# Decode block on one core: the stored row as one transfer of two rows, V in four loads, b1 in two

## The chip, the cores and the metric

The kernel runs on one core of one Trainium2 chip. The metric is the device time of one execution in microseconds (us). A profile of one execution is at hand as well; its *span*, from the first to the last instruction, is a little shorter than the time that is measured for that same execution.

## What is computed

One token `x` of 1024 numbers goes through an attention block over a sliding window and, beside it, through a small feed-forward block; both results are added to `x`.

```python
xn = layernorm(x)                                   # 1024
# A: 32 query heads of 128, 4 key/value heads, the last W = 4096 rows of the caches
q  = (xn @ wq)                                      # wq: 1024 x 4096
p  = softmax(q . k_cache[:, Sk-W:] / sqrt(128))     # K window: 4 x 4096 x 128
o  = p @ v_cache[:, Sk-W:]                          # V window: 4 x 4096 x 128
A  = o.reshape(4096) @ wo                           # wo: 4096 x 1024
# B
h  = gelu(layernorm(xn) @ w1 + b1)                  # w1: 1024 x 3584, b1: 3584
B  = h @ w2 + b2                                    # w2: 3584 x 1024
out = x + A + B                                     # 1024 numbers, bfloat16
```

All inputs are bfloat16. Every weight and both cache windows are read once: about 39.9 MB in all, for one token.

## The kernel before

The whole kernel is one straight program without loops at run time. All large inputs come over SyncE's (SP's) DMA queue, in this order: K in four loads of 1 MB, one for each key head (L76); wq in two loads of 4 MB (L85); w1 in one load of 7 MB (L200); V in three loads, the first with two heads (2 MB) and the others with one (L208); w2 in one load of 7 MB (L214); wo in one load of 4 MB and five smaller ones of 2 MB down to 256 KB (L222). ScalarE's (ACT's) own DMA queue carries four small loads near the start: x in two layouts (L107, L108), b2 (L109) and b1 as eight rows of 448 numbers, 896 bytes each (L110). The tile `b1_8` that receives b1 is read by two matmuls at L238, which put b1 into the accumulator `acch` before the products with w1 (L243) are added there.

SBUF holds only part of the weights at a time, so the loads wait for one another's buffers. The pool `big` has two buffers of 64 KB per partition: the first takes K and the first half of wq (`kq`), and later w1 (`w1t`); the second takes the transposed K (`kt2`), and later w2 (`w2t`). The pool `ring` has two buffers of 32 KB: the second half of wq and V, then the two halves of wo. So w1 is issued when the first half of the wq products (L231, the 32 matmuls that read `kq`) is done; w2 when the scores (L260) are done; the second half of wo when `o_all` (L296, 32 matmuls on V) is done.

The stages in order: VectorE (DVE) transposes K block by block (L185) and moves the blocks together with ACT (L194, L196). TensorE (PE) makes q (L231), turns it (L247), makes the scores (L260); then come the maximum, the exponential (L275), the feed-forward's first product (L243) and GELU (L288), the product with V (L296), and at the end one long chain of 112 matmuls and a tail of 16 that accumulate w2 and wo rows into the result (L323, L340). The result lies as two rows of 512 numbers, in partitions 0 and 32. DVE and ACT write them to the tile `res` (L344, L345), and they are stored by two DMAs of one row each, one issued by SP (L347) and one by ACT (L348). At the end SP waits until every DMA has reported (L374), and the engines meet in a barrier.

Two things set the order of the work that the source leaves open:

- The framework's planner orders each engine's instructions ahead of time. It goes through the program with its own estimate of when things are ready, and an engine takes, of what is ready by that estimate, what stands first in the source. So the two matmuls of L238, which stand behind L231 in the source, run ahead of it; and L247 and L260 run ahead of L243, which stands before them. On the chip every engine then runs its instructions strictly in the order planned.
- DMAs issued by SP and ACT report on eight completion counters, handed out in turn over both queues, in the planned order. A DMA is not issued before the DMA that used its counter last, eight places ahead, has landed. The order is: K (4 loads), x, x, b2, b1, then wq (2), w1, V (3), w2, wo (6), and the two stores. So the two loads of wq wait for the first and the second load of K, although their buffers are free.

Of the kernel before, what the change touches and what calls it, by code (L numbers as in the profile page):

```python
# [15 lines left out]
def kernel(  # L16
# [14 lines left out]
    nc = tc.nc  # L31
    P = 128
    D = A_x.shape[-1]
    Hkv = A_k_cache.shape[1]
    Sk = A_k_cache.shape[2]
# [5 lines left out]
    W = min(4096, max(256, Sk // 4))  # L41
# [24 lines left out]
    def big_tile(name):  # L66
        return big.tile([P, 2 * RING_ELEMS], BF16, tag="big", name=name, align_bytes=256)
# [35 lines left out]
    x32 = consts.tile([32, 32], BF16)  # L103
    xb8 = consts.tile([8, 256], BF16)
    b1_8 = consts.tile([8, NH], BF16)
    with tc.issue_after(first_exp.ins):
        nc.scalar.dma_start(out=x32[:], in_=x_flat.rearrange("(a n) -> a n", a=32))  # L107
        nc.scalar.dma_start(out=xb8[0:4, :], in_=x_flat.rearrange("(a n) -> a n", a=4))  # L108
        nc.scalar.dma_start(out=xb8[4:8, :], in_=B_b2.rearrange("(a n) -> a n", a=4))  # L109
        nc.scalar.dma_start(out=b1_8[:], in_=B_b1.rearrange("(a n) -> a n", a=8))  # L110
    zf = consts.tile([P, 512 + Hq], FP32)
    nc.gpsimd.memset(zf[:], 0.0)
    zeros = zf[:, 0:512]
# [73 lines left out]
    for R in range(4):  # L187
        for Cd in range(4):
            src = scr[32 * R:32 * R + 32, :, :].rearrange("p g (c a j) -> p g c a j", a=4, j=32)[:, :, :, Cd, :]
            dst = kT[32 * Cd:32 * Cd + 32, :, WQ4 * R:WQ4 * (R + 1)].rearrange("p g (c j) -> p g c j", j=32)  # L190
            moves.append((dst, src))
    for i, (dst, src) in enumerate(moves):
        if i % 3 == 2:
            nc.scalar.copy(out=dst, in_=src)  # L194
        else:
            nc.vector.tensor_copy(out=dst, in_=src)  # L196

    w1t = big_tile("w1t")
    w1v = w1t[:, :C * Fd].rearrange("p (r n) -> p r n", r=C)
    nc.sync.dma_start(out=w1v, in_=w1_v)  # L200
# [2 lines left out]
    q_sb = q_f.rearrange("p (b n) -> p b n", b=2)  # L203
    v_sb = ring_tile("v_sb")
    v4 = v_sb[:].rearrange("p (g c d) -> p g c d", g=Hkv, c=NCH)
    for g0, g1 in ((0, 2), (2, 3), (3, 4)):
        src = A_v_cache[0, g0:g1, Sk - W:Sk, :].rearrange("g (p c) d -> p g c d", p=P)
        nc.sync.dma_start(out=v4[:, g0:g1, :, :], in_=src)  # L208

    chunk_src = []  # L210
    w2_v = B_w2.rearrange("(p c) n -> p c n", p=P)
# [14 lines left out]
    for i, w3 in enumerate(wq_tiles):  # L226
        for r in range(4):
            c = 4 * i + r
# [19 lines left out]
    for b in range(2):  # L248
        src = qT_ps[:, b * 4:(b + 1) * 4, :].rearrange("p hh (th t f) -> p th t hh f", th=2, t=2)[:, :, :, :, 0]
# [93 lines left out]
    res = consts.tile([33, 512], BF16)  # L343
    nc.vector.tensor_tensor(out=res[:, 0:N1], in0=acct[0][0:33, :], in1=bulk[0][:], op=ALU.add)  # L344
    nc.scalar.copy(out=res[:, N1:512], in_=acct[1][0:33, :])  # L345
    out_v = out.rearrange("a b (t n) -> (a b t) n", t=2)
    nc.sync.dma_start(out=out_v[0:1, :], in_=res[0:1, :])  # L347
    nc.scalar.dma_start(out=out_v[1:2, :], in_=res[32:33, :])  # L348


# [28 lines left out]
```

## Time and profile before

| what | us |
|---|---|
| median of 3 runs (lowest, highest) | 101.81 (101.69, 101.94) |
| the profiled execution's own time | 101.68 |
| its span, first to last instruction | 100.0 |
| PE busy, 361 matmuls | 48.5 |
| DVE busy | 38.2 |
| ACT busy | 29.2 |
| DMA: 39.91 MB moved, mean over the span | 399 GB/s |

Busy times are of one execution. The share of a whole span says little about a single stage; which wait ends last in a stage says more. About 1.7 us of the execution's time lie outside the span (101.68 against 100.0).

### The profile page before, as it was taken

Reading aid. Unit: us, or ns where it says so; the run is one execution under the profiler, and the core shown is the slowest. Engines: PE = TensorE matmul, PEld = TensorE weight load, DVE = VectorE, ACT = ScalarE, POOL = GpSimd, SP = SyncE. Lnnn points to the kernel's source line nnn. Section 1 sums busy time; section 2 is a strip of 40 time slices with the busy share of each in tenths; the row PEclk is TensorE's granted clock in tenths of the full one; section 3 lists DMA queues with packets and bytes.
Section 4 is the critical chain, followed back from the end, with each engine's and each line's share of the span. In section 5 each row is a group of like instructions: output and inputs, shape, how many; then the busy total and the mean of one; then the engine's idle time right before and its main releaser. Section 6 shows DMA issues by size and latency. Waiting matters only on the chain.

```text
span 100.0 us, 913 instructions
## 1 busy us (share of the span) xinstructions
PE 48.5 (49%) x361; PEld 19.5 (20%) x361; DVE 38.2 (38%) x26; ACT 29.2 (29%) x34; POOL 8.6 (9%) x33
## 2 busy tenths in 40 slices
PE   0006400008500940089149407997100999999980
PEld 0003100002100300053126203342000234224320
DVE  0069999999999970010631051002400000000020
ACT  5306100007999999900150440000400000000010
POOL 7911560000000000000001000000000000000000
PEclk9999999999995555555966997599755569999997
DMA  2999999999999888998599998998899999999910
GB/s 26 387 420 431 456 502 459 446 433 433 420 420 577 367 367 367 482 620 367 213 420 436 426 534 390 459 620 351 367 413 393 420 420 420 420 426 415 398 53 1
DMA packets 2663, 39.91 MB, mean 399 GB/s; under 512 B 338, under 2 KB 356, under 8 KB 740
## 3 DMA queue, kind: packets, MB, share of 16 engines
q1 hardware_dynamic: 2578, 39.85, 93.5%
q8 instruction: 3, 0.05, 0.2%
q10 hardware_dynamic: 82, 0.01, 0.1%
HBM read 39.86 MB, written 0.00 MB: 399 GB/s over the span
## 4 chain that ended last, share of the span: by engine, by line
DMA 80%; PE 14%; SPq 2%; issue 1%; DVE 0%
DMA v_sb<-in_A_v_cache_dram 33%; DMA wo<-in_A_wo_dram 25%; DMA kq<-in_A_wq_dram 17%; PE o_all L296 9%; DMA kq<-in_A_k_cache_dram 5%; PE accq L231 4%; SPq L222 1%; PE acct L340 1%; SPq L208 1%; DVE res L344 0%; PE acct L336 0%; SPq L200 0%
## 5 line engine op out<-in xcount | busy, mean ns | idle before, releaser
L194 ACT COPY kt<-kt 32x4096 bf16<-32x4096 bf16 x5 | 18.0, 3602 | 10.4 <-DVE kt L185 10.3
L185 DVE STREAM_TRANSPOSE kt<-kq 128x4096 bf16<-128x4096 bf16 x4 | 17.4, 4413 | 5.8 <-DMA kq<-in_A_k_cache_dram 5.8
L196 DVE COPY kt<-kt 32x4096 bf16<-32x4096 bf16 x11 | 13.4, 1219 | 0.2
L323 PE MATMUL accf<-w2t 128*1 128x512 bf16 x56 | 8.3, 466 | 5.7 <-DMA w2t<-in_B_w_dram 5.7
L296 PE MATMUL o_all<-v_sb,w1t 128*32 128x512 bf16 x32 | 8.8, 442 | 4.3 <-DMA v_sb<-in_A_v_cache_dram 4.3
L329 DVE COPY bulk<-accf 33x320 f32<-33x320 f32 x1 | 0.5, 482 | 24.7 <-ACT bulk L328 24.7
L231 PE MATMUL accq<-kq,xnT 128*1 128x512 bf16 x32 | 3.6, 627 | 10.2 <-DMA kq<-in_A_wq_dram 10.2
L323 PE MATMUL accf<-wo,o 128*1 128x512 bf16 x56 | 7.5, 378 | 0.1
L328 ACT COPY bulk<-accf 33x192 f32<-33x192 f32 x1 | 0.3, 312 | 23.2 <-PE accf L323 23.2
L231 PE MATMUL accq<-wq,xnT 128*1 128x512 bf16 x32 | 3.6, 626 | 6.1 <-DMA wq<-in_A_wq_dram 6.1
L231 PEld LDWEIGHTS <-xnT 128*1 128x1 bf16 x64 | 2.1, 116 | 20.5 <-issue 20.5
L296 PEld LDWEIGHTS <-w1t 128*32 128x32 bf16 x32 | 3.4, 109 | 9.6 <-DVE w2t L291 4.7
L323 PEld LDWEIGHTS <-w2t 128*1 128x1 bf16 x56 | 2.8, 98 | 10.8 <-issue 8.7
L243 PE MATMUL acch<-w1t,yT 128*1 128x448 bf16 x64 | 4.5, 450 | 0.0
L299 DVE TENSOR_TENSOR o_m<-o_all,grs 32x512 f32<-32x512 f32 x1 | 0.7, 678 | 9.0 <-PE o_all L296 9.0
L139 PE MATMUL x_ps<-x,zb 32*128 32x8 bf16 x4 | 0.2, 162 | 7.9 <-DMA x<-in_A_x_dram 7.9
L247 PE MATMUL qT_ps<-zb,w1t 128*128 128x128 bf16 x8 | 1.0, 311 | 6.2 <-ACT w1t L233 6.2
L303 ACT CAST o_bf<-o_f 32x128 bf16<-32x128 f32 x1 | 0.3, 297 | 12.5 <-DVE o_f L301 12.5
L291 DVE STREAM_TRANSPOSE w2t<-w1t 128x896 bf16<-128x896 bf16 x1 | 1.7, 1700 | 5.7 <-ACT w1t L288 5.7
L260 PE MATMUL sp<-kt,zb 128*32 128x512 bf16 x32 | 3.7, 631 | 0.3 <-DVE zb L252 0.3
L321 PE MATMUL spare<-zf,ident_f 128*1 128x512 f32 x8 | 3.6, 592 | 0.0
L323 PEld LDWEIGHTS <-o 128*1 128x1 bf16 x56 | 2.6, 82 | 4.3 <-issue 1.1
(78 smaller groups left out, 40.3 us busy)
## 6 DMA issues: line engine op xcount, KB each, us to landing
w1t<-in_B_w_dram SPq DMA_DIRECT2D x1, 7168.0 KB, 24.3
w2t<-in_B_w_dram SPq DMA_DIRECT2D x1, 7168.0 KB
kq<-in_A_k_cache_dram SPq DMA_DIRECT2D x4, 1024.0 KB, 8.1
kq<-in_A_wq_dram SPq DMA_DIRECT2D x1, 4096.0 KB, 17.1
wq<-in_A_wq_dram SPq DMA_DIRECT2D x1, 4096.0 KB, 24.1
wo<-in_A_wo_dram SPq DMA_DIRECT2D x1, 4096.0 KB
v_sb<-in_A_v_cache_dram SPq DMA_DIRECT2D x1, 2048.0 KB, 28.6
v_sb<-in_A_v_cache_dram SPq DMA_DIRECT2D x2, 1024.0 KB, 30.6
```

The source lines that it names most:

```text
L185: nc.vector.transpose(out=scr[:, g, :], in_=k2[:, g, :])
L194: nc.scalar.copy(out=dst, in_=src)
L196: nc.vector.tensor_copy(out=dst, in_=src)
L208: nc.sync.dma_start(out=v4[:, g0:g1, :, :], in_=src)
L222: nc.sync.dma_start(out=tv[:, a:b, :], in_=wo_v[:, nr * i + a:nr * i + b, :])
L231: nc.tensor.matmul(accq[32 * t:32 * t + 1, b, :], lhsT=xnT[:, c:c + 1], rhs=w3[:, r, j * 512:(j + 1) * 512], start=(c == 0), stop=(c == C ...
L243: nc.tensor.matmul(acch[32 * t:32 * t + 1, b, :NH], lhsT=yT[:, c:c + 1], rhs=w1v[:, c, j * NH:(j + 1) * NH], start=False, stop=(c == C - 1 ...
L260: nc.tensor.matmul(sp[32 * R:32 * R + 32, a, :], lhsT=qm[:, g, :], rhs=kT[:, g, c0:c0 + 512], start=(g == 0), stop=(g == Hkv - 1), tile_po ...
L291: nc.vector.transpose(out=hT, in_=h_sb.rearrange("p (d c) -> p c d", c=CW2))
L296: nc.tensor.matmul(o_all[:].rearrange("h g d -> h (g d)"), lhsT=eTb[:, 32 * c:32 * c + 32], rhs=v4[:, :, c, :], start=(c == 0), stop=(c == ...
L321: nc.tensor.matmul(spare[0:1, :], lhsT=ident_f[:, 0:1], rhs=zeros, start=True, stop=True)
L323: last = nc.tensor.matmul(accf[32 * half:32 * half + 1, :], lhsT=vec[kind](c), rhs=wap[:, half * 512:(half + 1) * 512], start=False, stop= ...
```

## The change

The result is stored by one DMA from SP that takes partitions 0 and 32 of `res` as two rows; the store from ACT goes. V is loaded by four loads of one head each instead of three. b1 is loaded by two DMAs of four rows: the first from ACT as before, the second from SP, and in the source it stands just ahead of w1's load.

```diff
     b1_8 = consts.tile([8, NH], BF16)
+    b1_v = B_b1.rearrange("(a n) -> a n", a=8)
     with tc.issue_after(first_exp.ins):
         nc.scalar.dma_start(out=x32[:], in_=x_flat.rearrange("(a n) -> a n", a=32))
         nc.scalar.dma_start(out=xb8[0:4, :], in_=x_flat.rearrange("(a n) -> a n", a=4))
         nc.scalar.dma_start(out=xb8[4:8, :], in_=B_b2.rearrange("(a n) -> a n", a=4))
-        nc.scalar.dma_start(out=b1_8[:], in_=B_b1.rearrange("(a n) -> a n", a=8))
+        nc.scalar.dma_start(out=b1_8[0:4, :], in_=b1_v[0:4, :])
...
+    nc.sync.dma_start(out=b1_8[4:8, :], in_=b1_v[4:8, :])
     w1t = big_tile("w1t")
     w1v = w1t[:, :C * Fd].rearrange("p (r n) -> p r n", r=C)
     nc.sync.dma_start(out=w1v, in_=w1_v)
...
-    for g0, g1 in ((0, 2), (2, 3), (3, 4)):
-        src = A_v_cache[0, g0:g1, Sk - W:Sk, :].rearrange("g (p c) d -> p g c d", p=P)
-        nc.sync.dma_start(out=v4[:, g0:g1, :, :], in_=src)
+    for g in range(Hkv):
+        nc.sync.dma_start(out=v4[:, g, :, :], in_=A_v_cache[0, g, Sk - W:Sk, :].rearrange("(p c) d -> p c d", p=P))
...
     out_v = out.rearrange("a b (t n) -> (a b t) n", t=2)
-    nc.sync.dma_start(out=out_v[0:1, :], in_=res[0:1, :])
-    nc.scalar.dma_start(out=out_v[1:2, :], in_=res[32:33, :])
+    nc.sync.dma_start(out=out_v, in_=res[0:33:32, :])
```

## The prediction

> **What bounds the kernel now.** I read the page first, then the chain that ended last, then a table of stretches, SP's own issues and waits, and last the start and the end of the timeline. From the page, the slices and the DMA queues:
>
> ```profile
> span 100.0 us, 913 instructions
> DMA  2999999999999888998599998998899999999910
> q1 hardware_dynamic: 2578, 39.85, 93.5%
> q8 instruction: 3, 0.05, 0.2%
> q10 hardware_dynamic: 82, 0.01, 0.1%
> ```
>
> The 16 DMA engines are full from the second slice to the 38th. SP's queue (q1) alone takes 93.5% of their time over the whole span. The table of stretches says it again, its last two columns being DMA share and GB/s:
>
> ```profile
> 3.00:26.00 23.00, 5.95 (x44) 2.68 (x45) 20.18 (x7) 5.61 (x14) 5.71 (x22) 1.00 1.04 445
> 26.00:36.00 10.00, 3.89 (x40) 0.94 (x31) 9.89 (x9) 9.96 (x4) 0.00 (x0) 0.72 0.92 400
> 36.00:60.00 24.00, 10.10 (x113) 5.76 (x109) 5.15 (x8) 10.24 (x9) 0.53 (x2) 0.69 1.03 441
> 60.00:95.00 35.00, 26.50 (x154) 9.54 (x156) 2.03 (x3) 1.12 (x4) 0.00 (x0) 0.80 0.99 422
> 95.00:100.00 5.00, 2.06 (x24) 0.60 (x20) 0.96 (x2) 0.62 (x2) 0.00 (x0) 0.87 0.08 25
> ```
>
> (The shares a little over 1 and 0.92 offset each other: long packets are booked where they start.) So from 3 to 95 us the time is the bytes. The chain of waits has steps that look like compute:
>
> ```profile
> 27.87 32.50 DMA v_sb<-in_A_v_cache_dram
> 60.50 8.77 PE o_all L296 x32
> 70.58 25.00 DMA wo<-in_A_wo_dram
> 95.62 0.60 PE acct L340 x8
> 97.22 0.48 DVE res L344
> ```
>
> The 8.77 us of `o_all` are in this chain only because they release the buffer of wo's last five loads. Those then wait 25 us behind w2 and the first half of wo, which are still in the queue; `o_all` could be many microseconds later at no cost. What sets the end is the stream of bytes, whose last landing is at 96.8, and the 3.2 us of the span (100.0 - 96.8) that follow it. An edit can move the time in three ways: it makes the stream longer, lets it run dry, or changes what follows it. The stream runs dry if SP issues a load too late:
>
> ```profile
> 8.42 0.33 SPq L85 DMA_DIRECT2D wq<-in_A_wq_dram  x1
> 26.50 0.33 SPq L200 DMA_DIRECT2D w1t<-in_B_w_dram  x1
> 26.87 1.42 SPq L208 DMA_DIRECT2D v_sb<-in_A_v_cache_dram  x3
> 47.56 0.33 SPq L214 DMA_DIRECT2D w2t<-in_B_w_dram  x1
> 97.78 0.32 SPq L347 DMA_DIRECT2D out_dram<-res  x1
> ```
>
> wq's second load lands 24.1 us after its issue, at 32.5; w1 is issued at 26.50, 6 us ahead. That is the tightest margin: w2 (47.56) has until V's last landing at 60.4.
>
> **V in four loads.** One more issue on SP of 0.47 (1.42 / 3): it ends near 28.8 instead of 28.3, and SP has nothing to issue before 47.56, so it is hidden. In the stream, bytes and packets stay (rows of 8 KB either way, 1152 such packets in the trace with those of K and wo), and 16 completion writes of 9 ns are added, one for each engine. The cost of a boundary between loads is bounded from the rows: w1 lands at 50.8 (26.50 + 24.3), V's first 2 MB at 55.5 (26.87 + 28.6), so 4.7 or 2.35 for each MB; the two that follow land at 57.9 (27.36 + 30.6) and 60.37, 2.43 each. A boundary costs at most 0.08; the 9 ns packet is the lower end. I take 0.02, since engines' own landings in the middle of the 16 differ by only that.
>
> The Trainium skill's page "DMA: Bandwidth & Descriptors", section "Rules for kernel authors", says the opposite of splitting: coalesce many small transfers, below 64 KB one pays mostly overhead; its section "Anatomy of one DMA" puts the constant at about 2 us each (there for DMAs issued from GpSimd). By that, as an estimate, the added V load and b1 load would make the time 4 us longer. The 2.43 us between landings of 1 MB, in which the packets alone need 8 x 0.309 = 2.47 for each engine, contradict it for loads queued behind one another.
>
> **b1 in two.** ACT's issue of 0.33 becomes about 0.26 (L109 has four rows), on an engine that next waits for x. The other half goes into SP's queue behind wq. Its counter is the one of K's third load, which landed at 10.7, so SP issues it near 10.7 (0.33) and then reaches w1, for which it waits until 26.50 anyway: hidden. Four of the engines carry a packet of 41 ns and one of 9 ns more and four others less: -0.05 to +0.05 on the stream, and I take +0.03. What counts is when it lands: behind 8 MB of wq, near 32.6 instead of 9.3 for the whole of b1 now. Its only reader is L238:
>
> ```profile
> 9.78 0.92 PE L238 MATMUL acch<-b,zb 8*128 8x448 bf16 x2
> 12.12 0.59 PE L150 MATMUL ln_tot<-st,ones_f 128*128 128x2 f32 x2 [1.42 <-ACT sq L148]
> ```
>
> Today it sits early on PE, ahead of the second layernorm and of the wq products (22.88 and 32.56). The planner has to place it anew. It puts an instruction where its operands are due: L247 and L260 run at 42.4 and 43.7, ahead of L243, which comes first in the source but has to wait for w1. On SP the b1 half stands behind wq's second load, so it is due just after that, when the second 32 matmuls of L231 (first in the source) are ready as well. So I expect L238 behind them, at 36.1 (32.56 + 3.58), where PE is idle for 6.2 us until L247 at 42.37. Its 0.92 us are hidden there; 9.78 to 10.7, where it was, was idle time too, so nothing is gained.
>
> **One store.** The end today, from SP's waits and the timeline:
>
> ```profile
> 97.78 0.25 ACTq L348 DMA_DIRECT2D out_dram<-res  x1
> SPq L347 <- DVE res L344: 25.8, 1, 25.8
> SPq L374 <- DMA out_dram<-res: 0.7, 1, 0.7
> ```
>
> Both stores are issued together. In the trace's packets they go through one DMA engine, at 98.515 (ACT's) and 98.561 (SP's); they report at 98.90 and 99.08. SP checks the counters in turn, ACT's and then SP's; it is past the last check at 99.22. The new store issues from SP at 97.78 as well. Issue: 0.32 with one row; the nearest rows for a few rows are 0.26 (L109) and 0.57 (L108), the farthest end is 0.87 (a wo load); I take 0.32. From issue to report: 1.12 (ACT's) to 1.30 (SP's, behind the other); I take 1.25, as a single DMA has nothing ahead of it on its engine. Its counter is the next after those of today's stores, which is the last that SP checks: one step of 0.06 fewer behind the report. So -0.11, between -0.31 (issue 0.25, report after 1.12, one step) and +0.49 (issue 0.87, the report as late as today, one step fewer).
>
> The same page, section "Why a DMA increments its semaphore by 16 and not by 1", says that a DMA runs on the largest number of engines up to 16 that divides its slowest dimension: two for two rows, four for half of b1. q10's 82 packets agree: 49 rows, and 16 + 4 + 4 + 8 + 1 completion writes.
>
> **The sum.** 101.68 + 0.02 + 0.03 - 0.11 = 101.62 for the profiled execution. That lies 0.13 below the median of the runs, so 101.75 as a median. No change that can be told: a measurement of this kernel can tell about 0.3%, or 0.3 us.
>
> **Rivals.**
>
> - *L238 keeps its place* ahead of the wq products (slower). Then PE stands at L238 until 32.6, and behind it 0.59 of layernorm and 3.61 of L231, which release w1: 32.6 + 0.92 + 0.59 + 3.61 = 37.7 instead of 26.49. The queue is empty from 32; from SP's first issue (0.79) to the first packet (1.82) pass 1.0, so the stream stands from 32 to 38.7. 101.75 + 6.7 = 108.4. It decides once w1's issue falls behind about 31. For it: that is the place today, and the half lands 23 us later than b1 does now. Against it: the planner's rule as the trace shows it. 0.15.
> - *The store is dearer*: two rows take an issue like L108 or the wo load, and the time becomes up to 101.75 + 0.6 = 102.35. 0.10.
> - *Two late engines become one*: three fetches of 16 KB of instructions (q8) run through the DMA engines, 0.96 us each, at 48.8 and 69.2 and at the end. Two of the 16 engines report wo's last load at 96.8, the others by 95.7. If another program layout puts both fetches on one engine, 1 us more: 102.75. Nothing in the diff changes PE's count of instructions by more than a wait or two. 0.06.
> - *A fixed cost for each transfer*: each of the two added loads stops the stream for as long as the store takes from issue to report, 1.3 us: 101.75 + 2.6 = 104.35. Against it are V's landings. 0.03. (The two sections named above are the rule for this.)
> - *The end gains more*: all lower bounds of the store hold, and the half of b1 costs nothing: 101.75 - 0.31 = 101.45 or, with the spread between runs, 101.2. This is the only gain I see. 0.22.
> - *The change isn't what it says*: bytes, packets and order of the large loads are the same, so most of it is nothing; that is in my forecast.
>
> **How the numbers follow.** Forecast (no change) 0.44: 101.45 to 102.1. Faster 0.22, down to 101.2. Slower 0.15 + 0.10 + 0.06 + 0.03 = 0.34. A range from 101.2 to 102.9 holds 0.44 + 0.22 + 0.10 + 0.06 = 0.82 and leaves out the stall and the fixed cost.
>
> **What would show it.** Right: q1 with 2578 + 16 + 8 + 2 = 2604 packets and q10 with 82 - 8 - 2 = 72; L238 near 36 us, waiting for nothing long; w1 issued at 26.5; DMA share as today in every stretch up to 95; `o_all` still starting near 60.5; the store's report between 98.9 and 99.1. Wrong: L238 ahead of L231 and w1 issued near 37, with slices of the DMA row near 0; V's landings more than 2.5 us apart; or a last wo landing that is not at 96.8.

## The result, and the profile after

| kernel | median us (lowest, highest) | ratio to before, 95% interval |
|---|---|---|
| before | 101.78 (101.61, 101.94), 10 runs | |
| changed | 101.98 (101.90, 102.24), 10 runs | 1.0026 [1.0018, 1.0035] |

The change makes the kernel 0.2 us slower. That is inside the range that was given and below the 0.3% that was called the limit, but the interval leaves out 1: ten runs of each tell it from no change. The sum had pointed the other way, to -0.06.

The profiled execution after took 102.24, the highest of its ten. Its page, the slices and the queues:

```profile
span 100.4 us, 913 instructions
...
DMA  2999999999999889998699999988899998999900
...
q1 hardware_dynamic: 2604, 39.85, 93.2%
...
q10 hardware_dynamic: 72, 0.01, 0.1%
```

The stream is as full as it was, and the two packet counts, 2604 and 72, are those that the prediction worked out. SP's issues and, in the second fence, PE's start:

```profile
10.63 0.33 SPq L199 DMA_DIRECT2D b<-in_B_b_dram  x1
26.45 0.35 SPq L202 DMA_DIRECT2D w1t<-in_B_w_dram  x1
26.85 1.85 SPq L209 DMA_DIRECT2D v_sb<-in_A_v_cache_dram  x4
47.55 0.33 SPq L215 DMA_DIRECT2D w2t<-in_B_w_dram  x1
...
97.94 0.57 SPq L348 DMA_DIRECT2D out_dram<-res  x1
```

```profile
12.07 0.59 PE L151 MATMUL ln_tot<-st,ones_f 128*128 128x2 f32 x2 [2.27 <-ACT sq L149]
22.82 3.58 PE L232 MATMUL accq<-kq,xnT 128*1 128x512 bf16 x32 [10.16 <-DMA kq<-in_A_wq_dram]
32.51 3.58 PE L232 MATMUL accq<-wq,xnT 128*1 128x512 bf16 x32 [6.10 <-DMA wq<-in_A_wq_dram]
36.02 0.92 PE L239 MATMUL acch<-b,zb 8*128 8x448 bf16 x2
```

The half of b1 is issued at 10.63, and its two matmuls (L239 now) moved to 36.02, behind both halves of the wq products. w1 goes out at 26.45 as before. The only row that departs from what was expected is the last of SP's: the store's issue takes 0.57 us where one row took 0.32. The end of the chain that ended last, then one of SP's waits:

```profile
95.81 0.60 PE acct L341 x8
96.41 0.42 PE acct L337 x4
96.83 0.53 PE acct L341 x6
...
97.38 0.48 DVE res L345
```

```profile
SPq L374 <- DMA out_dram<-res: 0.8, 1, 0.8
```

The store begins 0.56 after the last DVE operation begins, just as before (97.94 - 97.38; 97.78 - 97.22). In the trace's completion counts it reports at 99.56, 1.62 after its issue began; before, the two stores reported 1.12 and 1.30 after theirs.

This profile's DVE operation also starts 0.16 later than the one before did (97.38 against 97.22). That can't be put down to the change: over the kernels below the same row starts anywhere from 97.07 to 97.38, in single profiles, and in e4, which has the same loads, at 97.15.

### The profile page after: what moved, and what is told of

Its sections match the earlier page's. It is cut to its first block, busy times and chain, and to the rows that moved or that the text cites. A ratio compares the mean times of both kernels' runs of the same rounds, so it can differ in the third digit from the quotient of the medians.

```text
span 100.4 us, 913 instructions
## 1 busy us (share of the span) xinstructions
PE 47.7 (48%) x361; PEld 19.6 (20%) x361; DVE 38.2 (38%) x26; ACT 29.2 (29%) x34; POOL 8.6 (9%) x33
## 3 DMA queue, kind: packets, MB, share of 16 engines
q1 hardware_dynamic: 2604, 39.85, 93.2%
## 4 chain that ended last, share of the span: by engine, by line
DMA 81%; PE 12%; SPq 2%; issue 1%; DVE 0%
DMA v_sb<-in_A_v_cache_dram 32%; DMA wo<-in_A_wo_dram 27%; DMA kq<-in_A_wq_dram 17%; PE o_all L297 7%; DMA kq<-in_A_k_cache_dram 5%; PE accq L232 4%; SPq L209 1%; PE acct L341 1%; SPq L223 1%; DVE res L345 0%; PE acct L337 0%; SPq L202 0%
## 5 line engine op out<-in xcount | busy, mean ns | idle before, releaser
L297 PE MATMUL o_all<-v_sb,w1t 128*32 128x512 bf16 x32 | 7.1, 379 | 3.9 <-DMA v_sb<-in_A_v_cache_dram 3.9
L244 PEld LDWEIGHTS <-yT 128*1 128x1 bf16 x64 | 3.1, 107 | 1.4
```

Of the source, the lines that this page charges most:

```text
L244: nc.tensor.matmul(acch[32 * t:32 * t + 1, b, :NH], lhsT=yT[:, c:c + 1], rhs=w1v[:, c, j * NH:(j + 1) * NH], start=False, stop=(c == C - 1 ...
L297: nc.tensor.matmul(o_all[:].rearrange("h g d -> h (g d)"), lhsT=eTb[:, 32 * c:32 * c + 32], rhs=v4[:, :, c, :], start=(c == 0), stop=(c == ...
```

## The experiments

All kernels of a group (e1 to e4, e5 to e7, e8 to e10) ran on one chip beside the kernel before, each group on another chip; the two probes ran once each. A number that serves all of them is the *ending*: from the start of the last DVE operation (`res`) to the end of the last instruction, read from one profiled execution of each kernel. It holds the store and nothing of the stream.

| kernel | result row(s) stored by | ratio to before | ending us |
|---|---|---|---|
| before | SP and ACT, one row each | | 99.97 - 97.22 = 2.75 |
| changed | SP, partitions 0 and 32 | 1.0026 | 100.39 - 97.38 = 3.01 |
| e1 store only | SP, partitions 0 and 32 | 1.0035 | 100.20 - 97.07 = 3.13 |
| e2 V only | as before | 0.9994 | 100.08 - 97.34 = 2.74 |
| e3 b1 only | as before | 0.9997 | 99.85 - 97.11 = 2.74 |
| e4 loads only | as before | 1.0003 | 99.94 - 97.15 = 2.79 |
| e5 store from ACT | ACT, partitions 0 and 32 | 1.0028 | 100.40 - 97.26 = 3.14 |
| e6 both from SP | SP, one row twice | 1.0012 | 100.10 - 97.18 = 2.92 |
| e7 neighbours | SP, partitions 0 and 1 | 0.9980 | 99.89 - 97.22 = 2.67 |
| e8 rows 31, 32 | SP, partitions 31 and 32 | 1.0003 | 99.81 - 97.15 = 2.66 |
| e9 rows 31, 32 | SP and ACT, one row each | 0.9995 | 100.12 - 97.37 = 2.75 |
| e10 change, rows 31, 32 | SP, partitions 31 and 32 | 0.9977 | 99.69 - 97.16 = 2.53 |

**Which part of the change costs.** Theory: the store. Rival: the loads, since the profile after showed V's last landing at 60.61 instead of 60.37 and wo's last at 96.99 instead of 96.84.

e1, the store alone:

```diff
-    nc.sync.dma_start(out=out_v[0:1, :], in_=res[0:1, :])
-    nc.scalar.dma_start(out=out_v[1:2, :], in_=res[32:33, :])
+    nc.sync.dma_start(out=out_v, in_=res[0:33:32, :])
```

> Only the store is changed (one DMA of two rows from SP); V and b1 as before. If the store is the whole cost: its issue on SP takes about 0.57 us again (0.32 before), the report comes 1.6 us after the issue begins instead of 1.3, one check of SP's is saved (0.06), and the kernel is 0.2 to 0.3 us slower than before (102.0 to 102.05); the last landing of wo stays within 0.1 of 96.8. If instead the loads are the cost (last landing 96.99 against 96.84, a late DMA engine): no change, 101.8, with an issue near 0.32. If the slow issue of the one profile was chance: issue 0.32 to 0.4 and no change.

Measured: 102.1, ratio 1.0035 [1.0022, 1.0049]. The timeline's end:

```profile
97.07 0.48 DVE L344 TENSOR_TENSOR res<-acct,bulk 33x320 bf16<-33x320 f32 x1 [0.68 <-PE acct L340]
97.21 0.31 ACT L345 CAST res<-acct 33x192 bf16<-33x192 f32 x1 [1.33 <-PE acct L340]
97.63 0.61 SPq L347 DMA_DIRECT2D out_dram<-res  x1
```

The stream ended early here (wo's last landing at 96.69), and the kernel is still slower: an issue of 0.61, a report 1.62 after it begins. The slow issue was no chance.

e2, V alone:

```diff
-    for g0, g1 in ((0, 2), (2, 3), (3, 4)):
-        src = A_v_cache[0, g0:g1, Sk - W:Sk, :].rearrange("g (p c) d -> p g c d", p=P)
-        nc.sync.dma_start(out=v4[:, g0:g1, :, :], in_=src)
+    for g in range(Hkv):
+        nc.sync.dma_start(out=v4[:, g, :, :], in_=A_v_cache[0, g, Sk - W:Sk, :].rearrange("(p c) d -> p c d", p=P))
```

> Only V is changed (four loads of 1 MB); stores and b1 as before. If the store is the whole cost: no change (101.7 to 101.9), V's last landing within 0.1 of 60.4. If a boundary between loads costs: up to 0.08 us, 101.86. If the loads are what made the stream end 0.15 later: V's last landing near 60.6, the last of wo near 97.0, 101.95.

Measured: 101.66, ratio 0.9994 [0.9984, 1.0003].

e3, b1 alone:

```diff
+    b1_v = B_b1.rearrange("(a n) -> a n", a=8)
...
-        nc.scalar.dma_start(out=b1_8[:], in_=B_b1.rearrange("(a n) -> a n", a=8))
+        nc.scalar.dma_start(out=b1_8[0:4, :], in_=b1_v[0:4, :])
...
+    nc.sync.dma_start(out=b1_8[4:8, :], in_=b1_v[4:8, :])
     w1t = big_tile("w1t")
```

> Only b1 is changed (second half from SP's queue, ahead of w1). If the store is the whole cost: no change (101.7 to 101.9), L239 near 36 us as in the changed kernel. If the small transfer between wq and w1 costs the late engine its 0.2 us: w1 lands near 51.0 instead of 50.8 and the kernel takes 101.95 to 102.0.

Measured: 101.66, ratio 0.9997 [0.9985, 1.0009].

e4 has the edits of e2 and e3 together and the two stores of before.

> V in four and b1 in two, with the two stores of before: the changed kernel without its store. If the store is the whole cost: no change (101.7 to 101.9) and last landing 96.8 to 97.0 with no tie to the time. If the loads are the cost: 101.95 to 102.0, as the changed kernel.

Measured: 101.77, ratio 1.0003 [0.9992, 1.0015]. The loads cost nothing that can be told; the store is the whole of it. The rival has fallen, and with it the 0.15 by which the stream ended later in one profile: wo's last landing is at 96.96, 96.73 and 96.77 in e2, e3 and e4.

**What makes the store slow.** Three theories: its two rows; the 32 partitions between them; the fetch of 16 KB of instructions that runs through a DMA engine beside it (97.4 to 98.2 in the changed kernel). A probe puts six more stores behind those of before, each waiting for the one ahead:

```diff
     nc.scalar.dma_start(out=out_v[1:2, :], in_=res[32:33, :])
+    nc.sync.dma_start(out=out_v, in_=res[0:33:32, :])
+    nc.sync.dma_start(out=out_v, in_=res[0:2, :])
+    nc.sync.dma_start(out=out_v[0:1, :], in_=res[0:1, :])
+    nc.scalar.dma_start(out=out_v, in_=res[0:33:32, :])
+    nc.scalar.dma_start(out=out_v[0:1, :], in_=res[0:1, :])
+    nc.sync.dma_start(out=out_v, in_=res[0:33:32, :])
```

> The kernel before with six further stores behind its two, each of which waits for the one ahead to land, so that each is seen alone: from SP two rows (partitions 0 and 32), two rows (partitions 0 and 1), one row; from ACT two rows (0 and 32), one row; from SP two rows (0 and 32) again. Two of them store a row that isn't the result, and the last stores the result. If the shape makes the issue slow (two rows of a store): every two-row store takes 0.55 to 0.6 us to issue and about 1.6 to its report, every one-row store 0.25 to 0.32 and 1.1 to 1.3. If the distance of 32 partitions does it: only the stores of 0 and 32 are slow, 0 and 1 is like one row. If the fetch of instructions at 96.5 to 98.2 that runs beside the store does it: all stores here are fast, 0.25 to 0.33, whatever their shape.

Measured, in the timeline of SP and of ACT (start, duration of the issue):

```profile
97.69 0.32 SPq L347 DMA_DIRECT2D out_dram<-res  x1
99.06 0.58 SPq L349 DMA_DIRECT2D out_dram<-res  x1
100.74 0.26 SPq L350 DMA_DIRECT2D out_dram<-res  x1
101.91 0.23 SPq L351 DMA_DIRECT2D out_dram<-res  x1
105.98 0.51 SPq L354 DMA_DIRECT2D out_dram<-res  x1
```

```profile
97.70 0.25 ACTq L348 DMA_DIRECT2D out_dram<-res  x1
103.06 0.60 ACTq L352 DMA_DIRECT2D out_dram<-res  x1
104.73 0.24 ACTq L353 DMA_DIRECT2D out_dram<-res  x1
```

L349, L352 and L354 take partitions 0 and 32: 0.51 to 0.60, from SP and ACT alike, with no fetch near them (the last one ends at 98.17). L350 takes two rows of partitions 0 and 1: 0.26, like one row. From the start of the issue to the report the stores of 0 and 32 need 1.62, 1.65 and 1.56, the neighbours 1.15, one row 1.09 and 1.10. It is the distance, not the number of rows, not the issuer and not the fetch.

The same in the kernel itself, from ACT (e5), by two one-row stores from SP (e6) and with neighbouring partitions (e7):

```diff
-    nc.sync.dma_start(out=out_v[0:1, :], in_=res[0:1, :])
-    nc.scalar.dma_start(out=out_v[1:2, :], in_=res[32:33, :])
+    nc.scalar.dma_start(out=out_v, in_=res[0:33:32, :])        # e5
+    nc.sync.dma_start(out=out_v[0:1, :], in_=res[0:1, :])      # e6
+    nc.sync.dma_start(out=out_v[1:2, :], in_=res[32:33, :])    # e6
+    nc.sync.dma_start(out=out_v, in_=res[0:2, :])              # e7
```

> The kernel before, its two stores replaced by one of two rows from ACT. If the shape is the cost: as slow as from SP, 0.3 to 0.4 us over before (102.05), with an issue of 0.55 to 0.6. If SP is the slow issuer: issue near 0.25, time as before or 0.1 less. If the instruction fetch beside it is the cost: between the two, by where the fetch lies.

Measured: 102.03, ratio 1.0028 [1.0014, 1.0043], issue 0.58, report after 1.63. ACT is no better.

> The kernel before, its two one-row stores both issued from SP, one behind the other. If one-row issues cost 0.26 to 0.32 each and the report comes 1.0 us after the issue's end: the second report about 0.25 to 0.3 later than before, 101.95 to 102.05, as slow as the one store of two rows. If only the two-row shape is slow and issues overlap with what follows: within 0.1 of before.

Measured: 101.85, ratio 1.0012 [1.0000, 1.0025]. The issues took 0.32 and 0.26, the second began 0.36 behind the first and reported 1.10 after it began. The loss of about 0.1 is less than the 0.25 to 0.3 of the first expectation: the second issue is 0.36 later than SP's of before, but its report takes 1.10 instead of 1.30, 0.16 in sum, as in the ending (2.92 against 2.75). The 1.30 of before belongs to a store whose packet ran just behind ACT's (98.561 and 98.515).

> The kernel before, its two stores replaced by one of two rows from SP, but of partitions 0 and 1 (the second row stored isn't the result). If two rows are the cost whatever their distance: 0.3 to 0.4 us over before (102.05), issue 0.55 to 0.6. If the distance of 32 partitions is: issue 0.3 and no change, 101.7, or 0.1 less.

Measured: 101.6, ratio 0.9980 [0.9969, 0.9991], and in the timeline an issue like that of one row:

```profile
97.79 0.32 SPq L347 DMA_DIRECT2D out_dram<-res  x1
```

Its report came after 1.15: this one store of two rows beats the two stores. The kernel leaves the second result row out, so it shows the price of the shape and isn't a version to use. The two reports on the store's counter lie 0.02 apart (98.92, 98.94), where those of the two one-row stores lay 0.18 apart.

**Which distances.** The second probe stores rows of a constant tile `zb`, again one after the other, and at its end (not shown) the result rows again:

```diff
+    for s in (1, 2, 4, 16, 64):
+        nc.sync.dma_start(out=out_v, in_=zb[0:s + 1:s, 0:512])
+    nc.sync.dma_start(out=out_v, in_=zb[32:34, 0:512])
+    out_4 = out.rearrange("a b (t n) -> (a b t) n", t=4)
+    nc.sync.dma_start(out=out_4, in_=zb[0:4, 0:256])
+    nc.sync.dma_start(out=out_4, in_=zb[0:97:32, 0:256])
+    nc.sync.dma_start(out=zb[0:33:32, 512:1024], in_=out_v)
+    nc.sync.dma_start(out=zb[0:2, 512:1024], in_=out_v)
...
```

> The kernel before with stores from SP behind its two, each waiting for the one ahead, of a tile of constants (they are overwritten by the result at the end): two rows whose partitions lie 1, 2, 4, 16 and 64 apart, two neighbouring rows that begin at partition 32, four neighbouring rows, four rows 32 apart; then two loads of two rows, 32 apart and neighbouring; then one-row stores. If any distance over 1 makes the issue slow: 0.23 to 0.33 us for the neighbours wherever they begin, 0.5 to 0.6 for 2, 4, 16 and 64, for four rows 32 apart and for the load 32 apart. If only distances of a whole 32 partitions do: 2, 4 and 16 are fast, 64 is slow. If it is a matter of stores: the load 32 apart is fast. If the time goes with the rows: four rows 32 apart take about twice the addition of two (0.8 to 0.9).

Measured, in SP's timeline, a window for each store: distances 1, 2, 4, 16 and 64.

```profile
99.16 0.25 SPq L350 DMA_DIRECT2D out_dram<-zb  x1
100.36 0.73 SPq L350 DMA_DIRECT2D out_dram<-zb  x1
102.15 0.58 SPq L350 DMA_DIRECT2D out_dram<-zb  x1
103.77 0.58 SPq L350 DMA_DIRECT2D out_dram<-zb  x1
105.40 0.50 SPq L350 DMA_DIRECT2D out_dram<-zb  x1
```

Then, in one window over the rest of the probe, neighbours from partition 32 (L351), four neighbours (L353), four rows 32 apart (L354), and the loads of two rows 32 apart (L355) and neighbouring (L356):

```profile
106.94 0.24 SPq L351 DMA_DIRECT2D out_dram<-zb  x1
108.09 0.26 SPq L353 DMA_DIRECT2D out_dram<-zb  x1
109.26 0.59 SPq L354 DMA_DIRECT2D out_dram<-zb  x1
110.97 0.54 SPq L355 DMA_DIRECT2D zb<-out_dram  x1
112.86 0.25 SPq L356 DMA_DIRECT2D zb<-out_dram  x1
```

Every distance over 1 costs about 0.25 to 0.5 more issue, 2 no less than 64, loads as stores, and four rows no more than two. The reports come 1.53 to 1.77 after the issue begins for the distant stores, 1.13 to 1.16 for the neighbours; for the loads 1.87 and 1.25. So the whole addition is 0.4 to 0.65: part of it is in the issue, the rest between the issue's end and the first packet. The store's counter narrows it down: it is updated once ahead of any packet, 0.41 to 0.47 after the issue begins where the partitions are neighbours (both probes, e7, e8, e10) and 0.92 to 1.14 after it where they are not (both probes, the changed kernel, e1, e5). So nearly the whole addition lies ahead of that update. What is done in that time the trace doesn't show.

**A version with neighbouring rows.** PE writes the second result row to partition 32. If the first row's weights are loaded as 32 columns, the last of which is the vector, its product lands in partition 31 (the 31 rows above it hold sums that nobody reads), and the two rows are neighbours:

```diff
-    vec = {"h": lambda c: hT[:, c, 0:1], "o": lambda c: o8[:, c:c + 1]}
+    hx = w2t[:, CW2 * D - 31:CW2 * (D + 32)]
+    vec = {"h": lambda c, half: hx[:, 32 * c + 31 * half:32 * c + 32], "o": lambda c, half: o8x[:, c + 31 * half:c + 32]}
+    rows = (slice(0, 32), slice(32, 33))
...
-            last = nc.tensor.matmul(accf[32 * half:32 * half + 1, :], lhsT=vec[kind](c),
+            last = nc.tensor.matmul(accf[rows[half], :], lhsT=vec[kind](c, half),
...
-    nc.sync.dma_start(out=out_v[0:1, :], in_=res[0:1, :])
-    nc.scalar.dma_start(out=out_v[1:2, :], in_=res[32:33, :])
+    nc.sync.dma_start(out=out_v, in_=res[31:33, :])            # e8; e9: two stores of one row
```

(`o8x` is `o8` behind 31 columns of zeros; the tail's matmuls and the selection that puts x and b2 in place are changed alike.) e10 is e8 with V in four loads and b1 in two.

> The kernel before, with the first half of the result made in partition 31 instead of 0 (its weights are loaded as 32 columns whose last is the vector; the other rows of the product aren't read), so that the two result rows lie in neighbouring partitions 31 and 32, and are stored by one DMA of two rows from SP. If neighbouring partitions are what makes a two-row store cheap: issue 0.26 to 0.32, report 1.15 after it begins, time as of the store of partitions 0 and 1, ratio 0.998 (101.55 to 101.6), provided the wider weights cost nothing on PE, which waits for wo. If the wider weights slow the last matmuls: 101.7 or more. If 31 to 32 counts as a crossing of a quarter: issue 0.5 to 0.6 and 102.05.

Measured: 101.76, ratio 1.0003 [0.9992, 1.0013]. The issue is that of one row, as for partitions 0 and 1, but the time that was expected with it, a ratio of 0.998, didn't come:

```profile
97.71 0.32 SPq L351 DMA_DIRECT2D out_dram<-res  x1
```

> The same with partitions 31 and 32, but stored by two DMAs of one row as before. It isolates the wider weights: if they cost nothing, ratio 1.000 (101.7 to 101.8); if they do, it is as much over 1 as the kernel with one store is over 0.998.

Measured: 101.69, ratio 0.9995 [0.9986, 1.0005]: the wider weights cost nothing that can be told.

> The changed kernel (V in four, b1 in two, one store from SP) with the result rows in partitions 31 and 32. If the distance of 32 partitions is the whole cost of the change: 0.3 to 0.4 us less than the changed kernel's 101.98, ratio to before 0.998. If a part of the cost is in the loads: 0.999 to 1.001.

Measured: 101.48, ratio 0.9977 [0.9965, 0.9988], clear of both kernels. Its timeline's end:

```profile
97.16 0.48 DVE L349 TENSOR_TENSOR res<-acct,bulk 33x320 bf16<-33x320 f32 x1 [0.88 <-PE acct L345]
97.30 0.31 ACT L350 CAST res<-acct 33x192 bf16<-33x192 f32 x1 [1.54 <-PE acct L345]
97.72 0.27 SPq L352 DMA_DIRECT2D out_dram<-res  x1
```

e8 has the fast store (report after 1.15, ending 2.66) but not the time that e7, with the same ending, has, and beside e9, with two stores on the same chip, it shows no gain (101.76 against 101.69). Its profile can't say why: the profiled execution took 101.53, the fastest of the twelve. A part of e10's lead over e8 is seen: SP checks the completion counters two by two, 0.06 a check. In e1 and e8 the store's counter is checked in the third check from the end; two more DMAs in the program, the added V load and b1 load, turn it to the last one in the changed kernel and in e10. That makes the endings 3.01 instead of 3.13 and 2.53 instead of 2.66, 0.12 and 0.13 less. So in the endings the added loads do help a single store, by their number alone. The other 0.15 between the medians of e8 and e10, and e8's 0.16 over e7 (on another chip), no profile here shows. That stays open.

## Why the prediction failed

- **What bounds the kernel**: held. Every kernel here but e8 moves with its ending. In the profile after PE had a higher granted clock (1.00 instead of 0.69 from 36 to 60 us) and `o_all` ended at 67.8 instead of 69.3, without any gain.
- **V in four loads** (0.02, hidden issue): held, as far as e2's interval can tell (-0.16 to +0.03 us). The estimate from the Trainium skill (page "DMA: Bandwidth & Descriptors", sections "Rules for kernel authors" and "Anatomy of one DMA", whose constant is given for DMAs issued from GpSimd) would have made it and b1's split 4 us dearer. The runs disagree: e4's interval leaves room for 0.15 us.
- **b1 in two** (hidden issue near 10.7, L238 behind the wq products at 36.1): held to 0.1 us, 10.63 and 36.02. The stall that was the rival on the slow side didn't come. Nor did the two late DMA engines become one: two report wo's last load at 96.93 and 96.99, the others by 95.6. (Of the three fetches read there as 0.96 us each, the one at the end took 1.42 in the profile before.)
- **One store** (-0.11): this is the step that failed, by its size and its sign. Two choices in it were wrong. The issue was taken as 0.32 from the one-row store, though the bounds held 0.57 and 0.87; it is 0.57 to 0.61. And the report was taken at 1.25 after the issue began, because a single DMA has nothing ahead of it on its engine. e7's 1.15 agrees with that reason, but the row that it was read from had one partition, and the store takes two that lie 32 apart: 1.62. So the sign that was named for this step, a report between 98.9 and 99.1, failed: it came at 99.56. The issue bound of 0.57 came from L108, for its few rows; the probe shows that four neighbouring rows take 0.26, so it was near the truth by luck.
- **One check fewer** (-0.06): held. In the changed kernel one step follows the store's check (99.57, then 99.64), before two did (99.09, 99.16, 99.22).
- **The sum**: with 1.62 in place of 1.25 the store's term is -0.11 + 0.37 = +0.26 and the sum +0.31 instead of -0.06; measured are +0.20 for the medians and +0.26 for the endings (3.01 - 2.75). The rival "the store is dearer" was the case, with 0.10 for a chance and up to 0.6 for a price. That the time fell inside the range, and inside the forecast's own 101.45 to 102.1, is luck: both are wider than the change. The gains in it were added up too high: the 1.12 from issue to report holds ACT's issue already, so the store's lower end is -0.24 and not -0.31, and "the end gains more" took that off 101.75, which had -0.11 of the store in it.
- **Two engines for two rows**, the other rule of the Trainium skill's page "DMA: Bandwidth & Descriptors" (section "Why a DMA increments its semaphore by 16 and not by 1"): the trace agrees, the store's counter is updated once at 98.93, ahead of the store's first packet (99.16), and then takes two reports, at 99.52 and 99.56.

## What to carry to other kernels

Nothing hid the issue of this kernel's last store, so its price has to be read from a row with the same access pattern, the distance between its partitions included, not only the same size. Two rows that lie apart, stored by one DMA, lose to two stores. Two rows in neighbouring partitions have the shorter ending (2.53 to 2.67 against 2.74 to 2.79), and in two of three kernels (e7, e10) the shorter time too; in e8 no gain could be told. Split loads behind one another in this full stream cost nothing that could be told. An edit behind the stream is judged by the time from the last landing to the end, and by several runs: the one profile of e8 was its best.

## What the runs showed of the hardware that was not expected

- A small DMA (two or four rows, 2 KB) whose partitions are not neighbours took 0.50 to 0.73 us to issue instead of 0.24 to 0.32, and reported 0.4 to 0.65 later. Distances of 2, 4, 16, 32 and 64 are alike, two rows and four, stores and loads, SP and ACT. Neighbours alone don't make an issue short: L108, four neighbouring rows at the kernel's start, took 0.57, and a load of wo 0.87. Why, no run here shows.
- Of two one-row stores issued together by SP and ACT, the second's packet starts 0.046 to 0.053 us behind the first's, just when that one has ended, and reports 0.17 to 0.18 behind it (seven profiles); that looks like one DMA engine, but the trace doesn't name it. The two rows of one store report 0.01 to 0.04 apart.
